# Linear attention ahead of a mixture of experts: the first batch's denominators from key sums of their own, and the second batch's loads around the first weights

## The chip, the cores and the metric

The kernel runs on one core of one Trainium2 chip. The metric is the device time of one execution in microseconds (us), and lower is better. A time is the median of several executions. A ratio is the mean time of one kernel's fast runs over the mean of the other kernel's fast runs in the same rounds on the same chip, with a 95% interval, so it is not quite the ratio of the medians quoted beside it. A profile is of one execution, and its span is about 1.7 us shorter than the device time of that execution.

## The reference, cut to what matters

```python
def _attn_ref(q, k, v):                    # 8 batches, 8 heads, 576 tokens, 64 wide
    def phi(x, c, s):
        r = np.maximum(x, 0.0)
        return np.concatenate([r * c, r * s], axis=-1)
    q_p, k_p = phi(q, cos_w, sin_w), phi(k, cos_w, sin_w)
    kv = np.einsum('bhsf,bhsd->bhfd', k_p, v)
    z = np.sum(k_p, axis=2)                # the key sums
    num = np.einsum('bhsf,bhfd->bhsd', q_p, kv)
    den = np.einsum('bhsf,bhf->bhs', q_p, z)[..., None] + 1e-06
    return num / den

def _moe_ref(x, w_gate, w1, w2):           # 4608 tokens, 512 wide, 8 experts of 1024
    ...                                    # P: exp of the gate's logits, balanced in 8 rounds
    for e in range(8):
        out += P[:, e:e + 1] * (np.maximum(x @ w1[e], 0.0) @ w2[e])
```

The attention of each batch makes 576 rows of x. The kernel computes the attention of batch b+1 while TensorE already runs the first expert on "block" b, which is 512 rows of x. Only at the very start has TensorE nothing but attention to do.

## The kernel before

Loads are issued in one list from GpSimd (POOL). Dummy matmuls (`keep_busy`) fill TensorE's waits. They depend on no data.

```python
        load(0, 1, "q")                    # load(0, 0, "q") came earlier
        for name in "kv":
            load(0, 0, name)
            load(0, 1, name)
        w0 = new_weights(wA)
        load_w1(w0, 0, 4, (0, 1))
        load(1, 0, "kv")
        load(1, 1, "kv")
        load_w1(w0, 0, 4, (2, 3))
        load(1, 0, "q")
        load(1, 1, "q")
        load_w2(w0, 0, 4)

        def keep_busy(n):
            for _ in range(n):
                te.matmul(
                    out=idle_ps[:, 0:P], lhsT=ones_sq[:], rhs=ones_sq[:], start=True, stop=True
                )
        ...
        keep_busy(80)
```

The first batch: v is copied beside a column of ones, so that one pass of matmuls (`sums_begun`) gives kv and the key sums z together. The denominators therefore wait for v. `attend` makes the rows of x.

```python
        for hk in range(HK):
            prep_q(0, hk)                  # q_p on VectorE (DVE)
            for i in range(3):
                turn(0, hk, i, True)       # transposes on TensorE, relu on ScalarE (ACT)
        for hk in range(HK):
            prep_k(0, hk)
            prep_kp(0, hk)
        keep_busy(16)
        for half in range(2):
            prep_v(0, 2 * half, se.copy)
            prep_v(0, 2 * half + 1, (se.copy, ve.tensor_copy)[half])
            begun.append(sums_begun(0, half))
            keep_busy((4, 6)[half])
        sums_made(0, 0, begun[0])
        sums_made(0, 1, begun[1])
        epsilons(0)
        denominators(0)                    # 24 matmuls, then reciprocal, cast, hl on DVE
        keep_busy(34)
        ...
        for hk in range(HK):
            attend(0, hk)
            ...                            # batch 1's k_p between, then the first FFN matmuls
```

From batch 2 on, q is turned by the DMA. `at(j, s, ...)` puts work behind slot s of block j, a slot being one of the pieces of the block's FFN matmuls.

```python
        qp_pool = p1.enter_context(tc.tile_pool(name="qp_pool", bufs=3))
        ...
        def prep_q(b, hk):
            ...
            q_p = qp_pool.tile([P, C, 2, D], F16, name="q_p")
            ve.tensor_tensor(...)
            if by_dma:                     # b >= 2
                nc.sync.dma_start(out=qTs[b, hk], in_=q_p[:]..., transpose=True)
        ...
            if j == 0:                     # j: block; batch b = j + 1
                for half in range(2):
                    at(1, 0, load, b + 2, half)          # batch 3
            elif b + 2 < B:
                for half in range(2):
                    at(j, 11 + half, load, b + 2, half, "qkv", True)   # later: held back
```

The softmax here doesn't subtract the row's maximum and nothing guards it: scores larger than these inputs give would overflow.

Of the kernel before, what the change touches and what calls it, by code (L numbers as in the profile page):

```python
# [25 lines left out]
def kernel(  # L26
# [154 lines left out]
    with ExitStack() as p1:  # L181
# [50 lines left out]
            load(0, 1, name)  # L232
        w0 = new_weights(wA)
        load_w1(w0, 0, 4, (0, 1))
        load(1, 0, "kv")
        load(1, 1, "kv")
        load_w1(w0, 0, 4, (2, 3))
        load(1, 0, "q")
        load(1, 1, "q")
        load_w2(w0, 0, 4)  # L240

        def keep_busy(n):
# [21 lines left out]
        s_b = sval[:].unsqueeze(2).to_broadcast([P, C, D])  # L264
        se.activation(out=cs[:, :, 0, :], in_=s_b, func=AF.Sin, bias=half_pi[:], scale=-ang)
        se.activation(out=cs[:, :, 1, :], in_=s_b, func=AF.Sin, scale=ang)
        early = cs_pool.tile([P, 1], FP32, name="early")
        se.activation(out=early[:], in_=half_pi[:], func=AF.Exp)

# [55 lines left out]

        def prep_k(b, hk):
            k16 = loaded["k", b, hk]
            if b:
                se.activation(out=k16, in_=k16, func=AF.Relu)
            else:  # L330
                ve.tensor_scalar(out=k16, in0=k16, scalar1=0.0, scalar2=None, op0=ALU.max)
# [27 lines left out]
        def prep_kp(b, hk):  # L359
            k16 = loaded.pop(("k", b, hk))  # L360
            k_p = kp_pool.tile([P, C, 2, D], F16, name="k_p")
            ve.tensor_tensor(
                out=k_p[:], in0=k16.unsqueeze(2).to_broadcast([P, C, 2, D]),
                in1=cs, op=ALU.mult,
            )
            kps[b, hk] = (k_p, v_augs[(b * HK + hk) % len(v_augs)])

        def prep_v(b, hk, copy):
            copy(out=kps[b, hk][1][:, :, 0:D], in_=loaded.pop(("v", b, hk)))
# [1 line left out]
        def turn(b, hk, i, scalar=None):  # L371
# [17 lines left out]
            else:  # L389
                ve.tensor_scalar(  # L390
                    out=dst, in0=t_ps[:, 0 : C3 * P], scalar1=0.0, scalar2=None, op0=ALU.max
                )

        def sums(b, half):
            sums_made(b, half, sums_begun(b, half))

        def sums_begun(b, half):

            if half == 0:
                kvs[b] = (  # L400
                    kv_pool.tile([P, HK, 2, D], F16, name="kv_sb"),
                    kv_pool.tile([P, H, 32], F16, name="zsel"),
                )
            kv_ps = [ps_s.tile([P, 512], FP32, name="small_ps") for hh in range(2)]
            for i in range(2):
                k_p, v_aug = kps.pop((b, 2 * half + i))
                for c in range(C):
                    for hh in range(2):
                        te.matmul(
                            out=kv_ps[hh][:, i * (D + 1) : (i + 1) * (D + 1)],  # L410
                            lhsT=k_p[hh * HP : (hh + 1) * HP, c].rearrange("p a d -> p (a d)"),
                            rhs=v_aug[hh * HP : (hh + 1) * HP, c, 0 : D + 1],
                            start=(c == 0),
                            stop=(c == C - 1),
                        )
            return kv_ps

        def sums_made(b, half, kv_ps):
            kv_sb, zsel = kvs[b]
            for hh in range(2):  # L420
                kv_v = kv_ps[hh][:, 0 : 2 * (D + 1)].rearrange("p (hk d) -> p hk d", d=D + 1)

                def values():
                    se.copy(out=kv_sb[:, 2 * half : 2 * half + 2, hh, :], in_=kv_v[:, :, 0:D])

                if b:
                    values()
                ve.tensor_tensor(
                    out=zsel[:, 4 * half + hh : 4 * half + 4 : 2, :],
                    in0=zmask[:, 4 * half + hh : 4 * half + 4 : 2, :],  # L430
                    in1=kv_v[:, :, D : D + 1].to_broadcast([P, 2, 32]),
                    op=ALU.mult,
                )
                if not b:
                    values()

        den_pss = {}

        def epsilons(b):

            den_pss[b] = ps_s.tile([P, 512], FP32, name="small_ps")
            for j in range(3):
                te.matmul(
                    out=den_pss[b][32 * j : 32 * j + 32, 0 : C3 * HP],
                    lhsT=eps_row[:],
                    rhs=ones_col[0:1, :].to_broadcast([1, C3 * HP]),
                    start=True,
                    stop=False,
                )

        def denominators(b):

            zsel = kvs[b][1]
            den_ps = den_pss.pop(b, None)
            if den_ps is None:
                den_ps = ps_s.tile([P, 512], FP32, name="small_ps")
            for h in range(H):
                hk, hh = h // 2, h % 2
                for j in range(3):
                    te.matmul(  # L460
                        out=den_ps[32 * j : 32 * j + 32, 0 : C3 * HP],
                        lhsT=zsel[:, h, :],
                        rhs=qTs[b, hk][:, j * C3 : (j + 1) * C3, hh * HP : (hh + 1) * HP],
                        start=(h == 0 and b > 0),
                        stop=(h == H - 1),
                    )
            den = kv_pool.tile([96, C3 * HP], FP32, name="den")
            if b:
                ve.tensor_scalar(
                    out=den[:], in0=den_ps[0:96, 0 : C3 * HP], scalar1=1e-6 / XS,  # L470
                    scalar2=None, op0=ALU.add,
                )
                ve.reciprocal(out=den[:], in_=den[:])
            else:
                ve.reciprocal(out=den[:], in_=den_ps[0:96, 0 : C3 * HP])
            hi = kv_pool.tile([96, C3 * HP], F16, name="hi")
            ve.tensor_copy(out=hi[:], in_=den[:])
            hl = kv_pool.tile([96, C3 * HP], F16, name="hl")
            ve.scalar_tensor_tensor(
                out=hl[:], in0=hi[:], scalar=lo[0:96], in1=den[:], op0=ALU.mult, op1=ALU.add  # L480
            )
            hls[b] = hl
# [61 lines left out]


        begun = []
        for hk in range(HK):
            prep_q(0, hk)
            for i in range(3):
                turn(0, hk, i, True)  # L550
        for hk in range(HK):
            prep_k(0, hk)
            prep_kp(0, hk)
        keep_busy(16)
        for half in range(2):
            prep_v(0, 2 * half, se.copy)
            prep_v(0, 2 * half + 1, (se.copy, ve.tensor_copy)[half])
            begun.append(sums_begun(0, half))
            keep_busy((4, 6)[half])
        sums_made(0, 0, begun[0])  # L560
        sums_made(0, 1, begun[1])
        epsilons(0)
        denominators(0)
        keep_busy(34)

        hT = hA.tile([P, FT, TCH], F16, name="hT")
        first_ps = [
# [3 lines left out]
        ]  # L571
        for hk in range(HK):
            attend(0, hk)
            prep_k(1, hk)
            prep_kp(1, hk)
            if hk >= 2:
                prep_v(1, hk - 2, se.copy)
            for kt in ((), (0,), (1,), (2, 3))[hk]:
                for ft, h_ps in enumerate(first_ps):
                    te.matmul(  # L580
# [5 lines left out]
                    )  # L586
                    if kt == KT - 1:
                        se.activation(out=hT[:, ft, 0:TCH], in_=h_ps[:], func=AF.Relu)
        prep_v(1, 2, se.copy)
        prep_v(1, 3, ve.tensor_copy)  # L590

        for j in range(B):
            b = j + 1
            if j == 0:

                at(0, 4, prep_q, 1, 0)
                at(0, 4, lambda: begun.append(sums_begun(1, 0)))
                at(0, 5, lambda: sums_made(1, 0, begun[2]))
                at(0, 5, lambda: begun.append(sums_begun(1, 1)))
                at(0, 5, prep_q, 1, 1)  # L600
                for hk in range(HK):
                    for i in range(3):
                        at(0, 5 + hk, turn, 1, hk, i)
                    if hk == 0:
                        at(0, 5, lambda: sums_made(1, 1, begun[3]))
                    if hk < 2:
                        at(0, 5 + hk, prep_q, 1, hk + 2)
                at(0, 8, denominators, 1)
                at(0, 9, gates, 0)
                for hk in range(HK):  # L610
                    at(0, 11 + hk, attend, 1, hk)
            elif b < B:
                if j == 1:
                    for hk in (2, 3):
                        at(j, 0, prep_q, b, hk)
                        at(j, hk - 2, prep_kp, b, hk)
                        at(j, hk - 2, prep_v, b, hk, se.copy)
                    at(j, 1, sums, b, 0)
                    at(j, 3, sums, b, 1)
                else:  # L620
                    at(j, 0, sums, b, 1)
# [5 lines left out]
            if j == 0:  # L627
                for half in range(2):
                    at(j, 3, load, b + 1, half)
                for slot, fn, hk, *args in (  # L630
                    (11, prep_k, 0), (11, prep_q, 0), (12, prep_k, 1), (12, prep_kp, 0),
                    (12, prep_v, 0, se.copy), (13, prep_q, 1), (14, prep_k, 2),
                    (14, prep_kp, 1), (14, prep_v, 1, se.copy), (15, prep_k, 3),
                ):
                    at(j, slot, fn, b + 1, hk, *args)
            elif b + 1 < B:
# [537 lines left out]
```

## Time and profile before

| | before |
|---|---|
| device time, median (range) | 986.43 us (986.05 to 986.89, 3 runs) |
| TensorE busy, of a span of 984.8 us | 969.9 us |
| first attend begins | 23.16 us |
| block 1's first FFN matmul begins | 50.34 us |
| block 1's gate matmuls begin | 58.79 us |

The first part of the page gives the busy time of each engine, its share of the span, and its number of instructions:

```profile
span 984.8 us, 20226 instructions
...
PE 969.9 (98%) x7844; PEld 678.4 (69%) x7844; DVE 805.8 (82%) x1830; ACT 568.6 (58%) x1269; POOL 60.6 (6%) x82
```

TensorE (PE) has 15 us of gaps, and any gain must come from those or from slow stretches. The view of stretches shows the busy us and instruction count of each engine per stretch, then the TensorE clock that was granted (1.00 is full), the DMA share and GB/s:

```profile
10.00:15.00 5.00, 2.64 (x47) 2.10 (x46) 3.95 (x8) 3.85 (x10) 2.19 (x3) 1.00 1.26 201
15.00:20.00 5.00, 4.89 (x98) 3.49 (x93) 1.20 (x6) 1.61 (x6) 2.46 (x4) 0.57 1.28 204
20.00:25.00 5.00, 4.75 (x54) 3.93 (x48) 3.04 (x6) 1.47 (x4) 2.54 (x4) 0.75 1.33 201
...
55.00:60.00 5.00, 4.48 (x84) 2.54 (x77) 1.68 (x6) 2.98 (x8) 0.00 (x0) 1.00 0.73 77
```

TensorE is half idle up to 15 us, and then it is "busy" at little more than half the clock. DMA moves about 200 GB/s in these three stretches. The timeline gives the start, the duration, and the engine and work of each group. The bracket is the idle time of that engine before the group and what ended it:

```profile
14.60 1.03 PE L109 MATMUL small_ps<-acc_lo,k_p 64*128 64x65 f16 x36 [2.13 <-ACT acc_lo L109]
...
20.13 3.19 PE L109 MATMUL y_ps<-ones_sq 128*128 128x128 f16 x34
...
23.16 0.41 PE L109 MATMUL small_ps<-hl,acc_hi 96*128 96x192 f16 x3
...
58.52 0.35 PE L109 MATMUL small_ps<-q_pT,zsel 128*32 128x192 f16 x6 [0.52 <-DMA q_pT<-q_p]
58.79 0.66 PE L109 MATMUL small_ps<-wg,xT 128*128 128x8 f16 x20
```

The first line is the wait for v's copies. The 34 dummies from 20.13 cover the denominators' chain on DVE, whose last piece, `hl`, is the reciprocals in two fp16 parts that the attend multiplies with. The attend begins at 23.16. The line at 58.52 is a wait of half a microsecond for batch 2's transpose by DMA.

### The profile page before, as it was taken

Reading aid. Unit: us, or ns where it says so; the run is one execution under the profiler, and the core shown is the slowest. Engines: PE = TensorE matmul, PEld = TensorE weight load, DVE = VectorE, ACT = ScalarE, POOL = GpSimd, SP = SyncE. Lnnn points to the kernel's source line nnn. Section 1 sums busy time; section 2 is a strip of 40 time slices with the busy share of each in tenths; the row PEclk is TensorE's granted clock in tenths of the full one; section 3 lists DMA queues with packets and bytes.
Section 4 is the critical chain, followed back from the end, with each engine's and each line's share of the span. In section 5 each row is a group of like instructions: output and inputs, shape, how many; then the busy total and the mean of one; then the engine's idle time right before and its main releaser. Section 6 shows DMA issues by size and latency. Waiting matters only on the chain.

```text
span 984.8 us, 20226 instructions
## 1 busy us (share of the span) xinstructions
PE 969.9 (98%) x7844; PEld 678.4 (69%) x7844; DVE 805.8 (82%) x1830; ACT 568.6 (58%) x1269; POOL 60.6 (6%) x82
## 2 busy tenths in 40 slices
PE   8999999989999999999999999999999999999997
PEld 7545444447777777777777777777777777777775
DVE  5786774789889888988789888988888888988887
ACT  5776665467776555555555555555555555555551
POOL 6311110010000000000000000000000000000001
PEclk8999999999999999999999999999999999999999
DMA  9989990741013410133103400233103401104435
GB/s 162 206 122 162 157 151 9 136 77 47 34 41 68 85 32 25 49 68 68 49 25 69 91 25 25 56 62 67 49 25 68 92 25 27 47 26 117 128 87 129
DMA packets 80336, 73.54 MB, mean 75 GB/s; under 512 B 33264, under 2 KB 72176, under 8 KB 80240
## 3 DMA queue, kind: packets, MB, share of 16 engines
q0 software_dynamic: 27232, 30.94, 20.0%
q1 hardware_dynamic: 52768, 41.06, 17.2%
q8 instruction: 61, 1.00, 0.4%
q14 instruction: 35, 0.29, 0.1%
q10 hardware_dynamic: 240, 0.26, 0.1%
HBM read 83.12 MB, written 12.98 MB: 98 GB/s over the span
## 4 chain that ended last, share of the span: by engine, by line
PE 94%; DVE 2%; DMA 2%; ACT 1%; POOL 1%; issue 0%; POOLq 0%; ACTq 0%; SPq 0%
PE rows_ps L109 34%; PE h_ps L109 28%; PE copied_ps L109 11%; PE p_ps L109 11%; PE y_ps L109 6%; PE small_ps L109 4%; DMA v_ld<-in_v_dram 1%; DMA q_pT<-q_p 0%; DVE acc_hi L847 0%; POOL hs_last L862 0%; DVE P_tok L109 0%; DMA out_dram<-acc_lo 0%; DVE colp L109 0%; ACT u L109 0%; POOL k_ld L201 0%
## 5 line engine op out<-in xcount | busy, mean ns | idle before, releaser
L847 DVE SCALAR_TENSOR_TENSOR acc_lo<-rows_ps,P_tok,acc_lo 128x512 f32<-128x512 f32 (+1 forms) x322 | 203.1, 639 | 74.8 <-PE rows_ps L109 74.7
L109 PEld LDWEIGHTS <-H 128*128 128x128 f16 x2080 | 203.0, 98 | 83.1 <-issue 1.2
L783 ACT CAST u<-h_ps 128x384 f16<-128x384 f32 x288 | 137.6, 478 | 130.7 <-PE h_ps L109 130.7
L109 PEld LDWEIGHTS <-w1e 128*128 128x128 f16 x1632 | 156.4, 98 | 66.2 <-issue 6.0
L777 DVE CUSTOM_DVE_ANT_0 H<-p_ps,u 128x384 f16<-128x384 f32 x329 | 180.9, 550 | 6.7 <-PE p_ps L109 6.6
L109 PEld LDWEIGHTS <-hs 128*128 128x128 f16 x1500 | 146.6, 98 | 56.2
L109 PE MATMUL h_ps<-S,w1e 128*128 128x384 f16 x672 | 164.1, 326 | 1.1 <-ACT u L109 0.9
L109 PE MATMUL p_ps<-xT,T 128*128 128x384 f16 x672 | 164.1, 326 | 0.1
L109 PE MATMUL rows_ps<-V,H 128*128 128x256 f16 x1000 | 150.0, 273 | 0.7 <-DVE acc_hi L847 0.7
L109 PE MATMUL h_ps<-xT,w1e 128*128 128x384 f16 (+1 forms) x616 | 150.1, 350 | 0.2 <-DVE xT L109 0.2
L109 PE MATMUL rows_ps<-w2e,hs 128*128 128x256 f16 x1000 | 150.0, 273 | 0.0
L815 ACT ACTIVATE H<-h_ps 128x384 f16<-128x384 f32 x144 | 70.6, 490 | 95.1 <-PE h_ps L109 95.1
L109 PEld LDWEIGHTS <-T 128*128 128x128 f16 x1008 | 98.1, 98 | 29.5 <-issue 3.1
L109 PE MATMUL rows_ps<-w2e,H 128*128 128x256 f16 (+1 forms) x568 | 91.2, 285 | 0.0
L796 ACT COPY copied_ps<-h_ps 128x384 f32<-128x384 f32 x144 | 67.5, 469 | 36.0 <-PE h_ps L109 35.2
L806 ACT ACTIVATE H<-copied_ps 128x384 f16<-128x384 f32 x144 | 70.8, 492 | 20.4 <-PE copied_ps L109 20.4
L109 PE MATMUL h_ps<-S,T 128*128 128x384 f16 x336 | 81.8, 325 | 0.4 <-ACT copied_ps L109 0.3
L109 PE MATMUL copied_ps<-xT,w1e 128*128 128x384 f16 x336 | 82.1, 326 | 0.0
L109 PE MATMUL copied_ps<-w2e,H 128*128 128x256 f16 x504 | 75.5, 272 | 0.0
L109 PE MATMUL rows_ps<-V,hs 128*128 128x256 f16 x500 | 74.9, 272 | 0.0
L847 DVE SCALAR_TENSOR_TENSOR acc_lo<-copied_ps,P_tok,acc_lo 128x256 f32<-128x256 f32 x126 | 60.0, 476 | 0.4
L847 DVE SCALAR_TENSOR_TENSOR acc_hi<-rows_ps,P_tok,acc_hi 128x512 f32<-128x512 f32 (+1 forms) x56 | 41.3, 737 | 20.6 <-PE rows_ps L109 19.7
(140 smaller groups left out, 956.9 us busy)
## 6 DMA issues: line engine op xcount, KB each, us to landing
S<-x_saved SPq DMA_DIRECT2D x108, 192.0 KB, 2.4
out_dram<-acc_lo SPq DMA_DIRECT2D x62, 128.0 KB, 2.4
w1e<-in_moe_w_dram POOLq DMA_DIRECT2D x7, 1024.0 KB, 9.0
w2e<-in_moe_w_dram POOLq DMA_DIRECT2D x7, 1024.0 KB, 9.6
q_ld<-in_q_dram POOLq DMA_DIRECT2D x16, 288.0 KB, 7.4
k_ld<-in_k_dram POOLq DMA_DIRECT2D x16, 288.0 KB, 8.3
v_ld<-in_v_dram POOLq DMA_DIRECT2D x16, 288.0 KB, 9.4
x_saved<-S SPq DMA_DIRECT2D x18, 192.0 KB, 1.9
```

The lines of the kernel that those rows point to most:

```text
L109: i = getattr(self.engine, name)(*args, **kwargs)
L777: latest = ve._custom_dve(TENSOR_ADD_SAT, out=out, in0=ps[:, 0:TU], in1=t[:], s0=FP32_MAX, s1=0.0)
L783: se.copy(out=t[:], in_=ps[:, 0:TU])
L796: se.copy(out=Y[:, 0:TU], in_=X[:, 0:TU])
L806: se.activation(out=h11, in_=Y[:, 0:TU], func=AF.Relu)
L815: se.activation(out=h12, in_=X[:, 0:TU], func=AF.Relu)
L847: ve.scalar_tensor_tensor(out=a, in0=rows, scalar=P_tok[:, g, self.e : self.e + 1], in1=a, op0=ALU.mult, op1=ALU.add,)
```

## The change

The intent is to take the denominators off v's load. The key sums of batch 0 come from k alone, by two times 36 half-array matmuls of two columns. The moving tile `cs_half` holds cosines and sines with zeros for the other head, one column per head of a pair; one half of the array takes the cosines, the other the sines. The reciprocal then runs while v is still being summed. Dummies between the transposes are meant to keep the clock up (the profile of before has 0.57 of it in 15 to 20 us). Batch 1's k is loaded first, then w1's second half, then q and v, and batch 1's work on DVE and ACT moves behind the attends.

```diff
         load_w1(w0, 0, 4, (0, 1))
-        load(1, 0, "kv")
-        load(1, 1, "kv")
+        load(1, 0, "k")
+        load(1, 1, "k")
         load_w1(w0, 0, 4, (2, 3))
-        load(1, 0, "q")
-        load(1, 1, "q")
+        for name in "qv":
+            load(1, 0, name)
+            load(1, 1, name)
         load_w2(w0, 0, 4)
@@ prep_k
-            if b:
+            if b >= 2:
                 se.activation(out=k16, in_=k16, func=AF.Relu)
@@
+        def key_sums(half):
+            z_ps = ps_s.tile([P, 512], FP32, name="small_ps")
+            for i in range(2):
+                for c in range(C):
+                    for a in range(2):
+                        te.matmul(
+                            out=z_ps[a * D : (a + 1) * D, 2 * i : 2 * i + 2],
+                            lhsT=loaded["k", 0, 2 * half + i][:, c],
+                            rhs=cs_half[:, c, a, :],
+                            start=(c == 0),
+                            stop=(c == C - 1),
+                        )
+            return z_ps
... (key_sums_made: zsel from z_ps on DVE; sums of batch 0 then 64 columns wide, no copy of v)
@@ first batch
+        epsilons(0)
         for hk in range(HK):
-            prep_q(0, hk)
+            if hk == 3:
+                prep_k(0, 0)
+                prep_k(0, 1)
+                z_ps = key_sums(0)
+                prep_q(0, hk)
+                key_sums_made(0, z_ps)
+            else:
+                prep_q(0, hk)
             for i in range(3):
                 turn(0, hk, i, True)
-        ...
-        keep_busy(34)
+                keep_busy(3)
+        prep_kp(0, 0)
+        prep_kp(0, 1)
+        denominators(0, range(0, 4))
+        keep_busy(8)
+        for hk in (2, 3):
+            prep_k(0, hk)
+        z_ps = key_sums(1)
+        prep_kp(0, 2)
+        key_sums_made(1, z_ps)
+        prep_kp(0, 3)
+        keep_busy(5)
+        denominators(0, range(4, 8))
+        for half in range(2):
+            sums_made(0, half, sums_begun(0, half))
+            keep_busy((0, 18)[half])
@@ after the attends
+            for i in ((), (), (0,), (1, 2, 3))[hk]:
+                prep_k(1, i)
+                prep_kp(1, i)
+        for hk in range(3):
+            prep_q(1, hk)
... (batch 1's transposes, v copies and sums at later slots of block 0; some of batch 2's work moved)
```

## The prediction

> **What bounds the kernel now.** TensorE: 969.9 of 984.8 us busy (the page's first part), with about 15 us of gaps. From 40 us on, its matmuls run back to back (stretches of 5 us: 4.9 to 5.0 busy), so whatever is won before 40 us should stay won, and the change touches nothing else. The prologue is slow: real FFN work starts only at 25.1 us, and the first attend at 23.1 (timeline). The chain of waits there is: the v load lands at 13.86, copies of v by ACT, key-value sums, denominators, 34 dummy matmuls that cover the reciprocal, attend. The stretches show why this is slow: TensorE is idle from 12.5 to 14.6 us, and from 15.5 to 22.7 us its granted clock is 0.5. [...]
>
> **What the change does to the prologue.** The key sums come from k (landed at 10.1 and 13.0) alone, so the denominators and the DVE reciprocal, cast and hl (1.35 + 0.31 + 0.41 us) run beside v's load and the sums instead of after them. v's copies (0.67 us) go. Added: 72 half-array matmuls (estimate 1 to 1.3 us per half, from 16 gate matmuls in 0.54 us), 36 dummies between transposes (each group costs about what ACT needs per transpose, 0.39 us). My walk through the engines in written order: transposes end at 13.5 to 14, second key sums at 15 to 16, second denominators at 16.3 to 17, sums done at 18, hl at 18.7 to 19.5. First attend at about 19.2: 3.9 us earlier. The half-done clock loss disappears with it.
>
> **What comes back.** DMA is saturated to 50 us (about 205 GB/s), so loads don't move in total. w1's second half lands some 3 us earlier, and the attends lose ACT's relus and copies of batch 1 (0.4 us won). But batch 1's relu, k_p and q_p now stand on DVE behind the attends (3 x about 0.95 us, then q_p 0.7 each), so the first transposes of batch 1 wait about 1 us on TensorE; then ACT, with 8 transposed evacuations, 2 v copies and 3 relus, paces the sums of batch 1 (another 0.5 us or so). w2 (landing 30 to 35) is still in time. The DMA transposes of batch 2 still stand in a busy queue; the 0.5 us wait at 58 us may go or stay.
>
> **Sum.** -3.9 - 0.4 + 1.0 + 0.5 = about -3 us on the critical path, or 0.3%. Predicted 983.2 us, range 981.2 to 985.2. Faster by over 2%: 0.01; within 2%: 0.98; slower by over 2%: 0.01.
>
> **What would show it right.** The granted clock stays at 1.0 through 10 to 25 us; first attend near 19 us and the first FFN matmul near 21; a TensorE gap of about 1 us between 27 and 30 us before batch 1's first transposes, released by DVE's q_p; the first second-layer matmul about 35 to 36.5 us instead of 38.1; from there on, traces equal but for the shift.
>
> **What would make it wrong.** The clock still halves [...]: up to 3 us lost. The two-column matmuls are slower than estimated. DVE's start slips, since the copies into cs_half wait for ACT's sines (up to 0.6 us). The DVE and ACT queues behind batch 1 are better overlapped than I walk them (gain near 4.5), or stall longer (gain near 1).

-3.9 - 0.4 + 1.0 + 0.5 comes to -2.8, put as about -3. "Saturated" is its word for what the profile of before shows, 201 to 207 GB/s in every 5 us from 10 to 50 us.

## More of the kernel before

`qp_pool` has three buffers, so the fourth `q_p` can be written only when the first transpose has read its own. `ld` has four buffers, two per batch, so batch 3's loads become possible as soon as batch 1's are used up.

## The result, and the profile after

| | before | after |
|---|---|---|
| device time, median (range), 4 runs each in the same rounds | 986.51 us (986.05 to 986.89) | 986.62 us (985.83 to 987.48) |
| ratio of the means | | 1.0001 (0.9984 to 1.0019) |
| TensorE busy / span | 969.9 / 984.8 us | 968.6 / 985.7 us |
| first attend | 23.16 us | 20.65 us |
| second layer of block 0 begins | 38.12 us | 38.75 us |
| block 1's first FFN matmul | 50.34 us | 50.35 us |
| block 1's gate matmuls | 58.79 us | 58.91 us |

The time is the same. The range of the prediction (981.2 to 985.2) does not hold it. The first attend is 2.5 us earlier, and by 50 us nothing of that is left. The stretches after, in the columns of before:

```profile
10.00:15.00 5.00, 4.88 (x133) 4.21 (x130) 4.21 (x11) 2.97 (x8) 2.20 (x3) 1.00 1.24 190
15.00:20.00 5.00, 2.45 (x97) 2.06 (x96) 2.72 (x5) 0.87 (x4) 2.14 (x3) 1.00 1.31 202
20.00:25.00 5.00, 4.62 (x28) 2.25 (x27) 1.64 (x4) 1.40 (x4) 2.85 (x4) 0.66 1.31 204
```

The hole of 10 to 15 us is gone, as intended. A new one lies in 15 to 20, and the clock falls after it. The timeline shows where, and the later lines answer those of before:

```profile
15.50 1.22 PE L109 MATMUL small_ps<-v_ld,k_p 64*128 64x64 f16 x72
...
16.66 0.79 PE L109 MATMUL y_ps<-ones_sq 128*128 128x128 f16 x11
...
17.37 0.42 DVE L109 SCALAR_TENSOR_TENSOR hl<-hi,lo,den 96x192 f16<-96x192 f16 x1
...
20.27 0.55 PE L109 MATMUL y_ps<-ones_sq 128*128 128x128 f16 x7 [2.82 <-issue]
...
20.65 0.41 PE L109 MATMUL small_ps<-hl,acc_hi 96*128 96x192 f16 x3
...
31.95 0.68 PE L109 MATMUL small_ps<-ident,q_p 128*128 128x128 f16 x9 [0.76 <-DVE q_p L109]
...
54.46 1.02 PE L109 MATMUL h_ps<-xT,w1e 128*128 128x512 f16 x4 [0.57 <-ACT hT L109]
...
58.91 0.66 PE L109 MATMUL small_ps<-wg,xT 128*128 128x8 f16 x20
```

The 18 dummies ahead of the first attend run as 11, then nothing for 2.82 us, then 7. Dummies wait for nothing. What the attend needs (`hl`) was ready at 17.8. The bracket says "issue", which means that no semaphore, engine or DMA transfer shown in the profile held TensorE. The chain of waits (start, us, what) says the same:

```profile
16.73 0.72 PE y_ps L109 x11
17.45 2.82 issue
20.27 0.55 PE y_ps L109 x7
```

An engine that waits for nothing and still stands may be out of instructions; that is to be tested. The view of the DMA queues, restricted to 17.7 to 18.8 us, shows a packet of the instruction queue just there (columns: packets, MB, share of 16 engines):

```profile
q0 software_dynamic: 206, 0.21, 115.5%
q8 instruction: 1, 0.02, 5.4%
```

In the trace this packet has 16,384 bytes and moves from 17.78 to 18.72 us. When TensorE stops at 17.45, exactly 705 of its instructions are on record as started (LDWEIGHTS and MATMUL counted apart, and four semaphore and drain instructions with them). The same figure in the other kernels is what the first experiments look at.

Two theories stood at this point. Theory F: TensorE ran dry because its instruction fetch is slow while loads fill the DMA, and the change's 67 narrow dummies and its 72 key-sum and 72 value-sum matmuls, packed together, use up a block of instructions faster than the next arrives. Rival R: the hole belongs to the work, for example a hidden dependency of the dummies' PSUM tile on the denominators. (The recorded expectations call these A and B, and the later idea of a floor under batch 2's transposes E.) A second question was why a gain of 2.5 us at 20 us was gone at 50.

### The profile page after: what moved, and what is told of

The parts are those of the page before. It is cut to its first block, busy times and chain, and to the rows that moved or that the text cites. A ratio compares the mean times of both kernels' runs of the same rounds, so it can differ in the third digit from the quotient of the medians.

```text
span 985.7 us, 20379 instructions
## 1 busy us (share of the span) xinstructions
PE 968.6 (98%) x7923; PEld 677.0 (69%) x7923; DVE 805.8 (82%) x1833; ACT 565.3 (57%) x1263; POOL 60.6 (6%) x82
## 4 chain that ended last, share of the span: by engine, by line
PE 94%; DVE 2%; ACT 2%; issue 1%; POOL 0%; DMA 0%; ACTq 0%; SPq 0%; DVEq 0%; POOLq 0%
PE rows_ps L109 34%; PE h_ps L109 28%; PE copied_ps L109 11%; PE p_ps L109 11%; PE y_ps L109 6%; PE small_ps L109 4%; ACT acc_lo L109 0%; DVE k_p L109 0%; DVE acc_hi L900 0%; POOL hs_last L915 0%; DVE P_tok L109 0%; ACT hT L109 0%; DMA out_dram<-acc_lo 0%; DVE colp L109 0%; ACT u L109 0%
```

## The experiments

A quantity that puts all runs in order is the start of block 1's gate matmuls (53 to 62 us, and 68 in e3). The span less this start is 926.0 us before, 926.8 after, and between 925.7 and 926.8 in every kernel below except e6 to e9 and e13. So whatever the others win or lose is decided before that point.

### First look at the hole: e1, e2, e3, e5

e1 makes the first 80 dummies 20 of 512 columns: the same columns, with 120 fewer instructions (LDWEIGHTS and MATMULs) before everything else. (The late dummies show what width does to their time: 18 of 128 columns took 1.11 us in e1, and the same columns in five matmuls took 1.08 us in e2.)

```diff
-        def keep_busy(n):
+        def keep_busy(n, wide=1):
-            for _ in range(n):
+            while n:
+                m = min(n, wide)
+                n -= m
                 te.matmul(
-                    out=idle_ps[:, 0:P], lhsT=ones_sq[:], rhs=ones_sq[:], start=True, stop=True
+                    out=idle_ps[:, 0 : m * P].rearrange("p (m c) -> p m c", c=P),
+                    lhsT=ones_sq[:],
+                    rhs=ones_sq[:].unsqueeze(1).to_broadcast([P, m, P]),
+                    start=True, stop=True,
                 )
-        keep_busy(80)
+        keep_busy(80, 4)
```

> The changed kernel, but its first 80 dummies (128 columns each) are 20 of 512 columns: the same columns in 120 fewer TensorE instructions, nothing else moved. Theory A (TensorE runs out of instructions: the hole of 2.8 us at 17.45 us lies between dummies that wait for nothing, and a 16 KB block of the instruction queue moves at 17.78 to 18.72): the hole is at a place of the instruction stream, so with 120 fewer before it TensorE gets 120 further before it may starve; no hole at 17.45, first attend when hl is ready, near 17.9 us instead of 20.65; the clock stays 1.0 through 25 us; time 983.5 to 985.8. Rival B (the hole belongs to these dummies or to a wait that the trace does not show): the hole stays after the eleventh of the 18 dummies at about 17.45, time 986.6.

Measured: 985.59 us (985.32 to 986.77), ratio 0.9996 (0.9984 to 1.0009). The time is in the expected range, but a hole is still there. e2 has `m = min(n, 4)` for all dummies. (The recorded expectation miscounts: 147 dummies become 41, and the trace has 106 matmuls fewer, so 212 instructions.)

> The changed kernel with all its dummies in matmuls of up to 512 columns (147 become 44; 206 fewer TensorE instructions, the same columns). Theory A: no hole anywhere before 26 us, clock 1.0 throughout, first attend near 17.9 us. Theory A with C (behind the attends the second batch's work on DVE, ACT and its loads sets the pace): of the 2.8 us at the first attend only 1 to 2 reach the first batch's second layer; time 984 to 985.5. If A alone were all: 983 to 984. Rival B: hole stays, 986.6.

Measured: 986.47 us (985.1 to 988.61), ratio 1.0003 (0.9989 to 1.0017). The expected time (984 to 985.5) and the expected absence of any hole both missed. e3 takes the competition away: every load behind batch 0's v is issued only when `hl` has been made. It is slow on purpose.

```diff
-        load_w1(w0, 0, 4, (0, 1))
-        load(1, 0, "k")
-        ...
-        load_w2(w0, 0, 4)
@@ behind the first batch's last dummies
+        load_w1(w0, 0, 4, (0, 1), ve.last)
+        load(1, 0, "k", True)
+        ...
+        load_w2(w0, 0, 4, ve.last)
```

> The changed kernel, its dummies as they are, but all loads behind the first batch's v (w1, second batch's k, q, v, w2) are issued only when hl is ready, so the DMA queues are empty from about 15.3 to 18 us. Slower on purpose (w1 lands some 10 us later). It asks why the instruction block came late. Theory A1 (the fetch stands in the same DMA queues behind the loads): the block that moved at 17.78 us moves by 15.5 us, and the hole at 17.45 is gone or under 0.5 us. Theory A2 (the fetch is slow of itself, or starts only when TensorE has got to a certain instruction): block at 17 to 18 us and a hole as before.

Measured: 996.6 us, one look. (In the traces the fetch has a queue of its own, q8, beside q0 of the loads. What e3 tests is whether the loads delay it.) e5 undoes the second half of the change (batch 1's loads and order are those of before), with e2's dummies:

```diff
-        load(1, 0, "k")
-        load(1, 1, "k")
+        load(1, 0, "kv")
+        load(1, 1, "kv")
         load_w1(w0, 0, 4, (2, 3))
-        for name in "qv": ...
+        load(1, 0, "q")
+        load(1, 1, "q")
@@ prep_k
-            if b >= 2:
+            if b:
@@ attends and block 0: prep_k, prep_kp, prep_v, prep_q, turn, sums as in before
```

> Only the first batch's part of the change (denominators from own key sums, dummies between transposes), with all dummies wide; the second batch's loads, preparation and slots as in the kernel before. Theory C (the change's second half, which puts the second batch's relu, k_p and q_p behind the attends on DVE, gives back part of what the first half wins): this is faster than the wide version of the whole change, 982.5 to 984. Rival D (the second batch's loads, which land at the same times whatever is done, hold both): first transposes of the second batch no earlier than its q lands, about 28.5 us, and time within 0.7 us of the wide version of the whole.

Measured: 987.26 us (987.08 to 988.07), ratio 1.0012 (0.9999 to 1.0024), where 982.5 to 984 was expected. The holes, read from the traces ("instruction" counts TensorE's records up to the hole):

| kernel | hole, us | after instruction | what stands there | fetch packet begins |
|---|---|---|---|---|
| after | 17.45 to 20.27 | 705 | 12th of 18 dummies | 17.78 |
| e1 | 16.05 to 17.11 | 449 | 16th of 72 sums | 14.69 |
| e2 | 16.50 to 17.49 | 449 | 49th of 72 sums | 14.95 |
| e5 | 17.18 to 18.32 | 449 | 49th of 72 sums | 16.05 |
| e3 | none (0.18 us idle) | 705 | 12th of 18 dummies | 15.63 |

The timeline of e1 at its hole, and further on:

```profile
15.65 0.40 PE L109 MATMUL small_ps<-v_ld,k_p 64*128 64x64 f16 x15
17.11 1.00 PE L109 MATMUL small_ps<-v_ld,k_p 64*128 64x64 f16 x57 [1.06 <-issue]
...
53.37 0.76 DVE L109 TENSOR_TENSOR q_p<-q_ld,acc_hi 128x1152 f16<-128x1152 f16 x1 [2.00 <-DMA q_pT<-q_p]
...
54.86 0.46 PE L109 MATMUL small_ps<-acc_lo,k_p 64*128 64x65 f16 x18 [1.79 <-DVE k_p L109]
```

The timeline of e3, where the DMA queues are empty at that time:

```profile
17.30 0.79 PE L109 MATMUL y_ps<-ones_sq 128*128 128x128 f16 x11
...
18.26 0.55 PE L109 MATMUL y_ps<-ones_sq 128*128 128x128 f16 x7 [0.18 <-issue]
```

This settles against R that TensorE ran out of instructions. The hole follows the instruction count (449 and 705, which are 256 apart), not the work: it moves into the middle of the sums when 120 instructions are taken away. With the same instructions and no loads in the DMA (e3), it shrinks from 2.82 to 0.18 us. That the loads make the fetch late rests on e3, a single look. The packets of 16,384 bytes fit the distance of 256: over the whole span there is one for 256 to 257 of TensorE's instructions (62 packets on q8 for 15,846 LDWEIGHTS and MATMULs in after, 61 for 15,688 in before). Here the change of block is not hidden. In the profiled run of after, TensorE entered the block of instructions 450 to 705 at 14.07, the packet for the next block began to move 3.7 us later at 17.78, and its instructions ran from 20.27, 6.2 us after that entry. The change had used the block up in 3.2 us (14.07 to 17.23). In e3 the packet began 0.9 us after the entry, at 15.63. What asks for a block was not shown. Nor do the loads alone set the delay: from 10 to 45 us, with the DMA at 190 to 207 GB/s in every 5 us, the packets of before and after began 1.6 to 3.7 us after the first instruction of the block before (in before at 20.38, after 18.74; in after at 17.78, after 14.07). What sets it was not found.

The hole costs twice. The trace has the granted clock at one half from 21.51 to 24.92 us, 3.41 us, in which the attends and first FFN matmuls run (two of them take 1.03 us in place of 0.60). The half clock came behind a hole of 2.82 us. Further on, one came behind a wait of 1.90 us in e2 (from 55.27 to 58.69), while e1 kept its full clock through one of 1.79.

But e1 and e2 show that this is not the whole story. They attend at 19.07 and 18.93 and are at block 1's FFN at 47.54 and 47.41, almost 3 us ahead of after, yet they end within about 1 us of it. Here is the end of that lead in e1's chain of waits (start, us, what):

```profile
45.15 0.45 PE y_ps L109 x2
45.60 7.68 DMA q_pT<-q_p
53.28 0.03 issue
```

Batch 2's first q was given to the DMA to be turned at 45.60, and it landed 7.68 us later. The fourth `q_p` needs that buffer (DVE waits 2.00 us until 53.37), the fourth `k_p` stands behind it on DVE, and TensorE's sums stand behind that (1.79 us, until 54.86). The resume times hardly depend on the arrival: e1 arrives at 53.07 and resumes at 54.86, e2 resumes at 54.84 after 1.90 us, and e5 at 55.06 after 3.32 us. Whoever comes earlier waits longer. It is a floor at 55 us.

The packets show why. In e1 no packet of the transposes moves until 49.54 us, 3.9 us after the issue, while the loads keep queue 0 at about 190 packets per us. They speed up only when that queue empties at 51 to 52 us: the DMA of e1 moves 49 GB/s just before 52.1 us, and 228 to 299 from there to 53.7. From issue to landing a transpose took up to 7.8 us in e1, 9.4 in e10 and 10.1 in e5, and 3.3 to 3.5 in e14, where the loads were held back. After issues its first transpose at 48.4 (its first packet moves 1.3 us later) and reaches this place just as the floor lets go.

### Holding batch 3's loads: e6, e7, e8, e9

e6 is e1 with all six loads of batch 3 issued only after the last `q_p` of batch 2, so that the transposes find the DMA empty.

```diff
@@ block 1, batch 2
                         at(j, hk - 2, prep_v, b, hk, se.copy)
+                    for half in range(2):
+                        at(j, 0, load, b + 1, half, "qkv", True)
@@
-            if j == 0:
-                for half in range(2):
-                    at(1, 0, load, b + 2, half)
-            elif b + 2 < B:
+            if j and b + 2 < B:
```

> The changed kernel with the first 80 dummies wide (as in the run e1_first_wide) and the third further batch's loads (batch 3: q, k, v) issued only when DVE has made the last q_p of batch 2, instead of as soon as buffers are free. Theory E (in every run so far the loads end at 50.5 us and the DMA transposes of batch 2's q move no packet before 49 us, so TensorE goes on at 54.8 to 55.1 us however early it gets there: a floor that swallows what was won before): with those loads held the queues are empty near 42 us, each transpose lands within about 3 us of its issue, the gap of 2 us before the sums at 54.85 is gone, TensorE reaches the denominators of batch 2 near 55 us instead of 57.8, and the time falls to 982.5 to 984. Rival F (the transposes are slow of themselves, or the held loads are then late for batch 3): the gap stays or a new one of the same size opens at batch 3's relu between 53 and 60 us; time 985 to 987.

Measured: 989.64 us (987.82 to 989.73), ratio 1.0027 (1.0015 to 1.0039). e7 is e6 with a repaired order of batch 1: k's relu on ACT again, and `q_p` ahead of `k_p` on DVE.

```diff
-            if b >= 2:
+            if b:
@@
-            for i in ((), (), (0,), (1, 2, 3))[hk]:
-                prep_k(1, i)
-                prep_kp(1, i)
-        for hk in range(3):
-            prep_q(1, hk)
+            prep_k(1, hk)
+            if hk == 2:
+                prep_kp(1, 0)
+        prep_q(1, 0)
+        prep_q(1, 1)
+        prep_kp(1, 1)
+        prep_q(1, 2)
+        prep_kp(1, 2)
@@ slot 5
+                        at(0, 5, prep_kp, 1, 3)
```

> As e6_wide_hold3, and the second batch's work behind the attends in another order: relu of k on ACT after each attend instead of on DVE, and q_p made before k_p where the transposes need it first. Theory C (the wait of 1.25 us at 29.1 us for q_p, and the ACT queue to 35.2 us behind it, are the second loss): first transposes of batch 2 without a wait of TensorE over 0.3 us; first layer-two matmul 1.2 to 2 us earlier than in e6_wide_hold3; time 981.5 to 983, about 1.2 us under e6_wide_hold3. If loads hold that stage instead (rival: v of the second batch lands at 28 to 30 us, w2 at 31 to 35), no gain over e6_wide_hold3.

Measured: 989.52 us (987.51 to 989.87), ratio 1.0024 (1.0011 to 1.0037). e8 puts e6's hold on after, and e9 puts it on before.

> The changed kernel, dummies as they are, with batch 3's loads held as in e6_wide_hold3. It reaches batch 2's stage 2.8 us later than e1_first_wide because of the hole at 17.45 us, so the transposes cost it little: theories A and E together expect little, 0 to 0.7 us under the changed kernel (985.9 to 986.6). If the loads alone had taken the gain (and the hole nothing), it would fall to 983.5 to 984.5.

> The kernel before with batch 3's loads held in the same way. In its profile the transposes cost TensorE one wait of 0.5 us at 58 us. Theory E: 0.3 to 1 us under before (985.2 to 985.9); held loads that are late would show as a gap at 55 to 62 us and lose as much.

Measured: e8 992.98 us (991.39 to 994.03), ratio 1.0062 (1.005 to 1.0074). e9 991.19 us (986.61 to 993.73), ratio 1.004 (1.0022 to 1.0058). All four are losses, and all four expectations of a gain missed. The timeline of e6 tells why:

```profile
60.13 0.34 PE L109 MATMUL small_ps<-q_pT,zsel 128*32 128x192 f16 x6 [3.53 <-DMA q_pT<-q_p]
60.38 0.68 ACT L109 ACTIVATE k_ld<-k_ld 128x576 f16<-128x576 f16 x1 [4.61 <-DMA k_ld<-in_k_dram]
```

The stop at 53 to 55 us is gone (its sums run at 53.41), so the mechanism was right. But six loads of 288 KB, issued one after the other from 53.28 on, met the fourth transpose, which was issued at 53.53 and took 6.55 us where the first three took 3.25 to 3.48, and batch 3's k now comes late for ACT. The cure had been placed so that it made the same wait a little later.

e7's order did take away the wait for `q_p` before batch 1's transposes (the one at 31.95 in after), and it brought the second layer forward from 36.76 (e6) to 35.19, although part of this is its first attend at 18.77 in place of 19.89.

### Both repaired, and each alone: e10 to e14

e10 keeps the first 80 dummies narrow and makes all later ones wide. The idea: what matters is not only how many instructions there are but when TensorE begins a block of 256 and how long it takes over it (in after it took 3.2 us, and the next ran only 6.2 us after the start of this one). The narrow early dummies bring after to its 193rd instruction at 8.2 us, where e1 has 11.4, and wide late ones then stretch the next block.

```diff
-        def keep_busy(n):
+        def keep_busy(n, wide=4):
             ...                            # as in e1
-        keep_busy(80)
+        keep_busy(80, 1)
```

> The changed kernel; the first 80 dummies stay narrow and only the later ones (between and behind the transposes) become wide, the opposite choice to e1_first_wide. The traces so far say: TensorE stands at its 449th or 705th instruction, whichever comes before its block[...]. Narrow dummies at the start bring TensorE to instruction 193 at 8.3 us instead of 11.4, wide ones behind let the next 256 last longer than 5.8 us. So theory A expects no hole at all: none at instruction 449 (1.1 us in e1_first_wide) and none at 705 (2.8 us in the changed kernel), first attend at 17.6 to 18.2 us, clock 1.0 to 50 us. A plain count of instructions (fewer are better) would expect it worse than e1_first_wide. The time: still on the floor of batch 2's transposes, theory E, 985 to 986.5, with TensorE going on at about 54.8 us as in e1, e2 and e5.

Its 5.8 us was the estimate of the time from the 193rd instruction to the first of the block from 449: in e1 it was 5.7 us, from 11.4 to the resumption at 17.11.

Measured: 987.59 us (984.84 to 988.41), ratio 1.0006 (0.9992 to 1.002). The hole is gone, as expected; the time is above the expected 985 to 986.5. e11 is e10 plus a smaller hold: batch 3's first half is loaded as before, and only the second half waits, for DVE's last `k_p` of batch 2, by which time the fourth transpose is already under way.

```diff
@@ block 1, batch 2
+                    at(j, 1, load, b + 1, 1, "qkv", True)
                     at(j, 1, sums, b, 0)
@@
             if j == 0:
-                for half in range(2):
-                    at(1, 0, load, b + 2, half)
+                at(1, 0, load, b + 2, 0)
```

> As e10_late_wide, with the second half of batch 3's loads issued only when DVE has made batch 2's last k_p, after the fourth transpose is issued (in e6_wide_hold3 all six loads were held to a moment just before the fourth transpose; they stood before it and were late themselves). Theory E: the loads in front of the transposes end near 46 us instead of 50.5, no gap at 52 to 55 us and none over 0.5 us at the denominators; 983.3 to 984.8. Rival F (any holding makes batch 3 late): a wait for batch 3's k, q or v of the same size between 58 and 66 us, time 985.5 to 988.

Measured: 982.40 us (981.79 to 983.04), ratio 0.9959 (0.9946 to 0.9971), better than the expected 983.3 to 984.8. e12 is e11 with e7's order, e13 is before with e11's hold, and e14 is after with e11's hold and its dummies unchanged.

> As e11_late_wide_hold, with the second batch's order of e7_reorder (k's relu on ACT, q_p before k_p), which in e7_reorder brought the second layer 1.6 us forward. Theory: 982 to 983.8, over 1 us under e11_late_wide_hold, if the floor is gone; the same as e11_late_wide_hold if it is not.

> The kernel before with the second half of batch 3's loads held as in e11_late_wide_hold: what the holding alone is worth where nothing was won ahead of it. Theory E: it can only save the wait of 0.5 us at 58 us: 985.6 to 986.6. If it falls by over 1.5 us, the floor had bound the kernel before as much and the holding is a change of its own.

> The changed kernel with its dummies as they are and the second half of batch 3's loads held as in e11_late_wide_hold: the fourth corner of a square whose others are the changed kernel (986.6), e10_late_wide (987.6) and e11_late_wide_hold (982.4). If the hole at 17.45 us and the floor of the transposes were two independent losses, this would win the share of the holding alone; theory A with E says the two are in series: what the hole takes (2.8 us and then a stretch at half clock, 3 to 4 us by 46 us) is gone before the floor is reached, so the holding finds little to free: 985 to 986.5, hole at 17.4 us as before. If it comes near 983, the hole cost nothing.

Measured: e12 982.74 us (981.21 to 982.96), ratio 0.9958 (0.9946 to 0.9971), so its order gives nothing over e11 in total time, where over 1 us was expected. (Its profiled run attends 1.0 us later than e11's, at 18.56, and reaches the gate matmuls at 54.94, so about half a microsecond of that was made up.) e13 986.87 us (984.7 to 988.05), ratio 1.0003 (0.999 to 1.0015). e14 986.48 us (985.93 to 988.67), ratio 1.0011 (0.9999 to 1.0024).

| narrow dummies late (hole) | batch 3's loads at once (floor) | kernel | ratio to before |
|---|---|---|---|
| yes | yes | after | 1.0001 |
| no | yes | e10 | 1.0006 |
| yes | no | e14 | 1.0011 |
| no | no | e11 | 0.9959 |

Either repair alone is worth nothing, and together they are worth 0.4%. The two losses stand in series. The timeline of e10 shows a kernel without the hole (first attend at 17.42) running into the floor:

```profile
53.47 0.76 DVE L109 TENSOR_TENSOR q_p<-q_ld,acc_hi 128x1152 f16<-128x1152 f16 x1 [3.48 <-DMA q_pT<-q_p]
...
54.95 0.46 PE L109 MATMUL small_ps<-acc_lo,k_p 64*128 64x65 f16 x18 [3.28 <-DVE k_p L109]
55.35 3.55 PE L109 MATMUL h_ps<-xT,w1e 128*128 128x512 f16 x8
```

It waits 3.28 us, and behind this idleness the clock is halved once more (its trace has 0.5 from 55.43 to 58.84): the eight FFN matmuls take 3.55 us and not 1.90. An early arrival is punished beyond the wait itself. The timeline of e11, at the same places:

```profile
17.56 0.42 PE L109 MATMUL small_ps<-hl,acc_hi 96*128 96x192 f16 x3
...
51.12 0.75 PE L109 MATMUL small_ps<-acc_lo,k_p 64*128 64x65 f16 x36
51.80 1.90 PE L109 MATMUL h_ps<-xT,w1e 128*128 128x512 f16 x8
...
54.41 0.65 PE L109 MATMUL small_ps<-wg,xT 128*128 128x8 f16 x20
```

There is no hole, no half clock and no stop at the sums. The gate matmuls begin at 54.41 and not at 58.91, 4.5 us sooner. Its trace has no half clock until its last 0.2 us, and the mean granted clock of its five runs was 0.999 to 1.000, where nearly all runs of before have 0.994 to 0.998.

e14 is a clean test of the floor for after: its transposes are not disturbed, it has no stop for them, and it still reaches block 1's FFN at 50.20, since its hole is untouched (2.82 us of "issue" up to 20.23, as it is up to 20.58 in e8). e13 is less clean, and it is instructive. Up to the loads of batch 3, at 36 us, its instructions are those of before, but in its profiled run the clock was never halved there. The stretch and two lines of its timeline:

```profile
15.00:20.00 5.00, 4.92 (x126) 3.96 (x118) 2.89 (x8) 1.30 (x5) 2.87 (x4) 1.00 1.28 206
```

```profile
20.12 0.42 PE L109 MATMUL small_ps<-hl,acc_hi 96*128 96x192 f16 x3 [0.20 <-DVE hl L109]
...
57.41 0.35 PE L109 MATMUL small_ps<-q_pT,zsel 128*32 128x192 f16 x6 [2.50 <-DMA q_pT<-q_p]
```

It attends at 20.12, not 23.16 (e9 likewise, at 20.71), and is 3 us ahead at block 1's FFN (47.32). It then loses 2.5 us to the fourth transpose and runs at half clock until 61 us. So the half clock of 15.7 to 22.5 us that the profile of before shows is not in every execution. TensorE's idle time just ahead of it was 2.13 us in before and 1.24 in e13. In e13 and e9 the start that is some 3 us faster is eaten by a wait for the transposes. Among the runs of before, one of eleven in the second set had a mean clock of 1.000: it took 985.53 us against a median of 986.41. In e13 the held loads were issued from 52.27 us and their packets move from 54.82, while the fourth transpose (issued at 51.38) was under way. It landed after 5.99 us, where an undisturbed one took 3.2 to 3.5. What of its 2.5 us they caused is not separated, so e13 does not show that the kernel before, without the hold, would have lost as much.

### The first half of the change with both repairs: e15

e15 is e11 with the second half of the change undone as in e5 (the same diff, without the dummies).

> e11_late_wide_hold with the change's second half undone (the second batch's loads, relus, k_p, q_p and slots as in the kernel before). Where neither the hole nor the floor covers it, this shows what the second half is worth. Theory C (it costs, by the wait of 1 us for q_p and the ACT queue): 981.5 to 982.4, up to 1 us under e11_late_wide_hold. Rival: it pays, since w1's second half and q land 3 us earlier and ACT is freed in the attends: 983 to 984.5.

Measured: 981.25 us (981.09, 981.22, 981.25, 983.16, 983.92), ratio 0.9965 (0.9951 to 0.9978), just under the expected 981.5 to 982.4. Its timeline has

```profile
53.24 0.66 PE L109 MATMUL small_ps<-wg,xT 128*128 128x8 f16 x20
```

which is 1.2 us before e11, and from the first attend to block 1's FFN it takes 27.5 us (18.06 to 45.55) where e11 takes 28.5 (17.56 to 46.05). So in the trace the second half of the change costs about 1 us there. In total time e15 and e11 cannot be told apart (0.9965 and 0.9959, each against before in its own rounds), as e15's runs fall in two groups 2 us apart. No run here shows a use for the second half of the change.

## Why the prediction was right or wrong

**"The half-done clock loss disappears", key sums, dummies: right in the mechanism.** TensorE was busy 4.88 of the 5 us from 10 to 15 at a clock of 1.00, so the clock stayed full with the two-column matmuls and dummies in place of the idle time. A half's key sums took 0.73 and 1.01 us (1 to 1.3 predicted), transposes ended at about 12.5 (13.5 to 14), and `hl` was ready at 17.8 (18.7 to 19.5).

**"First attend at about 19.2": it came at 20.65. This is the step that failed first.** The walk through the engines in written order knew only waits for data, but TensorE stood for 2.82 us without instructions. The same instructions without loads in the DMA (e3) attended at 18.65, and with fewer late instructions (e10, e11) at 17.42 and 17.56. The walk was, if anything, too cautious. What it lacked was the instruction stream itself: the change adds 158 TensorE instructions (7923 matmuls against 7844, each with its LDWEIGHTS) and packs them closely into the time of heaviest loading.

**"The granted clock stays at 1.0 through 10 to 25 us": wrong.** It was 0.5 from 21.51 to 24.92, right behind the hole, and at no time in this stretch in e10 and e11, which have no hole. The first FFN matmul came at 22.90 and not near 21.

**"3.9 us earlier" was measured from a run of before with a half clock in its prologue.** The profile of before had it from 15.7 to 22.5. Such runs need not be rare: 29 of the 38 runs of before beside the experiments have a mean clock of 0.997, as the profiled run has, or less; where their half clock lies is not on record. The same instructions with a full clock attended at 20.12 (e13) and 20.71 (e9). From there, the first half of the change wins some 1.5 to 3.3 us once the hole is gone (first attends at 17.42 to 18.65 in e3, e10, e11, e12 and e15), not 3.9.

**"the first transposes of batch 1 wait about 1 us on TensorE": right.** The wait on `q_p` is 0.76 us at 31.95, and e15 against e11 gives about 1.0 us for the whole rearrangement, against the predicted 1.0 + 0.5 - 0.4 = 1.1. The second layer came at 38.75, not at 35 to 36.5, because the hole and the half clock came on top.

**"whatever is won before 40 us should stay won": the second step that failed, hidden behind the first.** In after itself it was hardly put to the test, since by the prediction's own mark, the second layer, 2.3 to 3.8 us were missing before 40 us (38.75 for 35 to 36.5). e10 tests it: its second layer begins at 34.55, ahead of the prediction, and its time is no better. The step was read from TensorE being 4.9 to 5.0 us busy in each 5 us after 40, although 55 to 60 us has 4.48. Such a reading says only that it does not wait at the present arrival time, not that it would not wait if it came earlier. e1, e2, e5 and e10 came earlier and waited 1.8 to 3.3 us at 55 us for `k_p`, behind `q_p`, behind a DMA transpose. With only the hole repaired, the kernel was no faster (987.59).

**"the 0.5 us wait at 58 us may go or stay": right object, wrong size.** Named as a doubt of 0.5 us, it was the visible edge of a floor worth up to 3.3 us, plus a half clock of 3.41 us in e2, e5 and e10, which waited 1.90 us or more.

**The sum.** The predicted -3 us exists: e11 is 4.1 us faster than before by medians (982.40 against 986.48), and it needs both repairs. That the size comes out near the forecast is partly luck, since the forecast had neither the two losses nor the half clock of before in it. In after itself, 2.5 us are won by 20.65. Of these, the half clock takes about 1.2 (after needs 8.65 us from its first attend to the FFN matmuls at 29.30, e11 7.44 for the same work) and the rearrangement about 1.0. For the remaining 0.3 us, gone by 50.35, no single wait was found. From there both kernels run alike: before waits 0.52 us for the transpose at 58.52, after 0.57 us for ACT at 54.46, and neither is early enough to meet more of the floor. So the failed steps give this account: the first term, -3.9, measured -2.5, the forecast had no term for the half clock (+1.2), and its +1.1 for the rearrangement came near the 1.0 measured.

**Left open.** Why about 1.5 us pass between the end of a fetch packet and the first use of its instructions (18.72 to 20.27), what sets the delay of a fetch packet under load, what asks for a block, and why the transposes' packets came only as the loads ran out, were not tested. Behind the gate matmuls, e6 to e9 lose a further 1 to 3.4 us and e13 1.5. Their traces have a half clock there, of 3.4 us in e6, e8 and e13 and of 6.8 us in e7 and e9. An estimate, half of its length, gives 1.7 and 3.4 us at most, so it can account for these losses.

## What to carry to other kernels

A stretch in which TensorE is fully busy does not prove that an earlier arrival will be kept: look for the releaser that comes last there (here a DMA transpose behind loads), and ask when it could have come. Count instructions as well as time where many short matmuls stand together under heavy DMA traffic, and make filler matmuls wide where a block of instructions has to last (here the later ones; with all of them wide, e2 still had a hole of 0.99 us). An idle gap whose releaser is "issue", in the middle of work that waits for nothing and at a fixed instruction number, was a fetch in this case. When two losses stand in series, each repair alone measures as nothing, so test them together before dropping either.
